# Tokens of tiles 4 to 7 transposed by DMA instead of TensorE, and the bulk of the weights issued behind them

## The chip, the core and the metric

The kernel runs on one core of a Trainium2 chip. A core has TensorE (PE: matmuls, with the weight loads that go before them, PEld), VectorE (DVE), ScalarE (ACT), GpSimd (POOL) and SyncE (SP), which issues nearly all DMAs here. Sixteen DMA engines move the data. The metric is device time of one execution in microseconds. Three runs of the kernel before took 226.38, 226.76 and 228.73 us, median 226.76.

## The reference

One layer on x of 2048 tokens by 512, bfloat16. xn is x normalised per token; to x are added a linear attention of xn with 32 heads of 16 and a gated bilinear block of xn:

```python
qkv = x @ wqkv                        # split into q, k, v of 32 heads of 16
phi = softmax(p), softmax(-p)         # p = q @ w_phi, or k @ w_phi, per head
kv  = phi_k^T v ;  z = sum_s phi_k    # over all tokens
o   = (phi_q kv) / (phi_q z + 1e-6)
A   = o @ wo
B   = ((x @ w_gate) * (x @ w_up)) @ w_down     # 512 -> 1792 -> 512
out = x + A(xn) + B(xn)
```

## The kernel before

The tokens are 16 tiles of 128. Everything stays on chip: x, the transposed normalised tokens xnT (features on the partitions, which matmuls need), all weights and the hidden values of the bilinear block.

**Tokens.** `ln` takes statistics on VectorE (L412, L414), the reciprocal root on GpSimd (L418, L420), and writes a normalised tile into a ring of four buffers, `xn_tile`, on VectorE (L434). That tile is then transposed into xnT. `emit_xn` does it in one of two ways: for tiles 0 to 7, four 128x128 matmuls against the identity into a PSUM bank (a "group") and one ScalarE copy out of it; for tiles 8 to 15, one DMA transpose issued from SP. A tile's buffer in the ring is free again when its transpose has read it.

**Keys and values.** `k_pe(t)` makes the values of a tile: four 128x512 matmuls and a ScalarE copy ("value group"). `wprime` folds w_phi into the key or query weights; it needs a weight matrix that a DMA transposes from HBM (`load_wT`, L344). `k_pk` and `k_norm` make the softmax features of the keys, with much work on VectorE (L474 and L480 for the maximum, L494 for the sums, L518, L521). `emit_kv` sums them over tokens. Later the queries go the same way, and their features and results are transposed by DMA from SP too.

**The bilinear block.** A *unit* is one of 14 slices of 128 hidden features for one of four groups of 512 tokens: a half of four 128x512 matmuls with gate, a half of four with up, a ScalarE copy of the first and a VectorE product (L543). Units 0 to 3 of a token group use the first 4 of 14 column blocks of gate and up, which are loaded early; units 4 to 13 use the other 10, the "bulk" of gate and up. Units 0 to 13 of the first token group need only tiles 0 to 3. The weights wd (w_down) and wo are used at the end, in `final`.

**Order of the work.** The program is first recorded as steps, and `_order` then sorts them by a list simulation of its own: each step has a cost, a DMA also a time `at` before which it does not count as landed, and among those ready on an engine the earliest, then that of the lowest priority number, is taken. Units have a high priority number, so they fill the gaps. The result is a fixed order for each engine. Each engine runs its list strictly in order and waits on semaphores where a step needs another engine's or a DMA's result. A dependence on a DMA is a wait for its landing. A change of a dependence, of a cost or of an `at` thus moves instructions on all engines.

**SP's queue before.** x in pieces of 1, 1, 2 tiles; the value weights wv; x of tiles 4 to 7; the first four blocks of gate and of up; the transposed load of the key weights; x of tiles 8 to 15; the bulk of gate (1280 KB) and up (1280 KB); wd (1792 KB); wo (512 KB); then the transposes of tiles 8 to 11. None of the loads waits for anything.

The functions that the diff touches:

Of the kernel before, what the change touches and what calls it, by code (L numbers as in the profile page):

```python
# [12 lines left out]
PE, ACT, DVE, POOL, SP = "PE", "ACT", "DVE", "POOL", "SP"  # L13
# [183 lines left out]
def _build(nc, es, A_x, A_wqkv, A_w_phi, A_wo, B_w_gate, B_w_up, B_w_down, out):  # L197
# [59 lines left out]
    def sbv(name, lo, n):  # L257
        off = layout[name] + lo
        return arena[:, off:off + n]
# [5 lines left out]
    def bank(b, lo=0, n=512):  # L265
        return psum[:, b * 512 + lo: b * 512 + lo + n]

    sc = _Sched(nc)


    def act_op(out_ap, in_ap, func=ACTF.Copy, scale=1.0, bias=None, prio=None):
        def fn(e):
            kw = {}
            if bias is not None:
                kw["bias"] = bias
            return e.activation(out=out_ap, in_=in_ap, func=func, scale=scale, **kw)  # L276
        r = [in_ap]
        if isinstance(scale, bass.AP):
            r.append(scale)
        if isinstance(bias, bass.AP):  # L280
            r.append(bias)
        return sc.step(ACT, fn, reads=r, writes=[out_ap], cost=(50.0 if str(in_ap.tensor.name) == "ps" else 95.0) + 0.833 * in_ap.free_size(),
                       lat=180.0, prio=prio)

    def dve(fn, reads, writes, n, rate=1.0, fixed=65.0, prio=None):
        return sc.step(DVE, fn, reads=reads, writes=writes, cost=fixed + rate * n / 0.96, lat=150.0, prio=prio)

    def pool(fn, reads, writes, n, rate=1.8, fixed=130.0, prio=None):
        return sc.step(POOL, fn, reads=reads, writes=writes, cost=fixed + rate * n, lat=120.0, prio=prio)

    def mms(items, prio=None, warm=False):

        def fn(e):
            ins = None
            for o, l, r, a, z in items:
                ins = e.matmul(o, lhsT=l, rhs=r, start=a, stop=z)  # L296
            return ins
        reads = []
        writes = []
        c = 0.0  # L300
        for o, l, r, a, z in items:
            reads += [l, r]
            writes.append(o)
            c += max(25.0, o.free_size() / 2.4 + 2.3) * (1.6 if warm else 1.0)
        return sc.step(PE, fn, reads=reads, writes=writes, cost=c, lat=260.0, prio=prio)
# [12 lines left out]
    def x_tile(t):  # L318
        return sbv("x", t * 512, 512)
# [8 lines left out]
    wo_v = sbv("wo", 0, NQ * 512).rearrange("p (q j) -> p q j", q=NQ)  # L328
    wg_v = sbv("wg", 0, NQ * FF).rearrange("p (q f) -> p q f", q=NQ)
    wu_v = sbv("wu", 0, NQ * FF).rearrange("p (q f) -> p q f", q=NQ)  # L330
    wd_v = sbv("wd", 0, NF * 512).rearrange("p (f j) -> p f j", f=NF)
# [3 lines left out]
    def load_x(on, t0, n, at):  # L335
        return sc.dma(on, sbv("x", t0 * 512, n * 512).rearrange("p (t d) -> p t d", t=n),
                      x_flat[t0 * 128:(t0 + n) * 128, :].rearrange("(t p) d -> p t d", p=128), at=at)

    def load_w(on, dst, src, at, issue=500.0):
        return sc.dma(on, dst, src, at=at, issue=issue)  # L340

    def load_wT(w, at):

        return sc.dma(SP, wT_v[:, w, :, :], A_wqkv[:, w * 512:(w + 1) * 512], transpose=True, at=at, issue=4600.0)  # L344

    def load_gu(on, f0, n, at):
        return [load_w(on, v[:, :, f0 * 128:(f0 + n) * 128],
                       src[:, f0 * 128:(f0 + n) * 128].rearrange("(q p) f -> p q f", p=128), at)
                for v, src in ((wg_v, B_w_gate), (wu_v, B_w_up))]

    sc.dma(ACT, wphi_v, bass.AP(tensor=A_w_phi.tensor, offset=A_w_phi.offset, ap=[[16, 128], [2048, NQ], [1, 16]]),
           at=4200.0)
# [5 lines left out]
    load_gu(SP, 0, 4, 10800.0)  # L358
    load_wT(1, 14000.0)
    load_x(SP, 8, 8, 17000.0)  # L360
    load_gu(SP, 4, 10, 24000.0)
    load_w(SP, wd_v, B_w_down.rearrange("(f p) j -> p f j", p=128), 30000.0)
    load_w(SP, wo_v, A_wo.rearrange("(q p) j -> p q j", p=128), 31500.0, issue=8000.0)


    zero = sbv("tree", 0, 128)
# [25 lines left out]
    def make_wbd():  # L392
        for jt in range(NQ):
            pool(lambda e, jt=jt: e.tensor_tensor(
                out=wbd_v[:, jt, :].rearrange("p (g f b) -> p g f b", g=2, b=4),
                in0=wphi_v[:, jt, None, :, None].to_broadcast([128, 2, 16, 4]),
                in1=bind8.rearrange("p (g b) -> p g b", g=2)[:, :, None, :].to_broadcast([128, 2, 16, 4]), op=ALU.mult),
                [bind8, wphi_v[:, jt, :]], [wbd_v[:, jt, :]], 128).deps.append(sc.by_eng[POOL][-2])


    stats_v = sbf("stats", 0, NT * 8).rearrange("p (t k) -> p t k", t=NT)
# [7 lines left out]
    def emit_ln_stats(t0, n):  # L409
        ts = slice(t0, t0 + n)  # L410
        for t in range(t0, t0 + n):
            dve(lambda e, t=t: e.bn_stats(stats_v[:, t, 0:6], x_tile(t)), [x_tile(t)], [stats_v[:, t, 0:6]], 512)  # L412
        for t in range(t0, t0 + n):
            dve(lambda e, t=t: e.bn_aggr(mv_v[:, t, :], stats_v[:, t, 0:6]), [stats_v[:, t, 0:6]], [mv_v[:, t, :]], 6)  # L414
        veps = lnt_v[:, 0, ts]
        var4 = mv_v[:, ts, 1:2]
        rstd4 = rstd_v[:, ts, 0:1]
        pool(lambda e: e.tensor_scalar(out=veps.unsqueeze(2), in0=var4, scalar1=1e-5, scalar2=None, op0=ALU.add),  # L418
             [mv_v[:, ts, :]], [veps], n)
        pool(lambda e: e.tensor_tensor(out=rstd4, in0=veps.unsqueeze(2), in1=mhalf[:, 0:n].unsqueeze(2), op=ALU.pow),  # L420
             [veps, mhalf], [rstd_v[:, ts, 0:1]], n, rate=155.0, fixed=400.0)

    def xn_tile(t):
        return sbv("xn", (t % 4) * 512, 512)
# [3 lines left out]
    def next_a():  # L428
        b = a_bank[0] % 5
        a_bank[0] += 1  # L430
        return b

    def emit_xn(t):
        dve(lambda e: e.tensor_scalar(out=xn_tile(t), in0=x_tile(t), scalar1=mv_v[:, t, 0:1],  # L434
                                      scalar2=rstd_v[:, t, 0:1], op0=ALU.subtract, op1=ALU.mult),
            [x_tile(t), mv_v[:, t, 0:1], rstd_v[:, t, 0:1]], [xn_tile(t)], 512, rate=0.5)
        if t >= 8:
            sc.dma(SP, xnT_v[:, :, t * 128:(t + 1) * 128], xn_tile(t), transpose=True, issue=1250.0, land=3200.0,
                   at=33000.0 + 1300.0 * (t - 8))
            return  # L440
        b = next_a()
        mms([(bank(b, q * 128, 128), xn_tile(t)[:, q * 128:(q + 1) * 128], ident, True, True) for q in range(NQ)])
        act_op(xnT_v[:, :, t * 128:(t + 1) * 128], bank(b).rearrange("p (q s) -> p q s", q=NQ))
# [106 lines left out]
    def emit_kv(half):  # L550
        for g in range(8):
            b = next_a()
            mms(group(bank(b, 0, 65), [(ek_v[:, t, g * 128:(g + 1) * 128], vext_all[:, t, g, 0:65])
                                       for t in range(half * 8, half * 8 + 8)]))
            kp = kvp_v[:, g, :]
            if half == 0:
                act_op(kp, bank(b, 0, 65))
                continue
            dve(lambda e, b=b, kp=kp: e.tensor_tensor(out=kp, in0=bank(b, 0, 65), in1=kp, op=ALU.add),  # L559
                [bank(b, 0, 65), kp], [kp], 65)  # L560
            dve(lambda e, kp=kp, g=g: e.tensor_tensor(
                out=kvx_v[:, g, 0:64].rearrange("p (h d) -> p h d", h=4),
                in0=kp[:, 0:64].rearrange("p (h d) -> p h d", h=4),
                in1=maskh[:, :, None].to_broadcast([128, 4, 16]), op=ALU.mult),
                [kp, maskh], [kvx_v[:, g, 0:64]], 64)
            dve(lambda e, kp=kp, g=g: e.scalar_tensor_tensor(
                out=kvx_v[:, g, 64:68], in0=maskh, scalar=kp[:, 64:65], in1=eps4, op0=ALU.mult, op1=ALU.add),
                [kp, maskh, eps4], [kvx_v[:, g, 64:68]], 4)
# [77 lines left out]
    def some_glu(n, g_max):  # L646
        for _ in range(n):
            if units and units[0][0] <= g_max:
                glu(*units.pop(0), (5, 6, 7) if units and units[0][0] < 3 else (5, 6))

    def ln(t0, n):
        emit_ln_stats(t0, n)
        for t in range(t0, t0 + n):
            emit_xn(t)
# [6 lines left out]
    for b0 in range(0, NT, 4):  # L661
        if b0 < 12:
            ln(b0 + 4, 4)
        if b0 == 8:
            load_wT(0, 0.0).deps.append(sc.by_eng[SP][-2])
            emit_kv(0)
            some_glu(99, 2)
        for t in range(b0, b0 + 4):
            k_pk(t)
            k_norm(t)  # L670
            if b0 < 8:
                some_glu(2, 1)
        if b0 < 12:
            for t in range(b0 + 4, b0 + 8):
                k_pe(t)
        if b0 == 8:
            wprime(0)
# [165 lines left out]
```

## Time and profile before

| | |
|---|---|
| median of three runs | 226.76 us |
| the profiled execution, its own time | 227.26 us |
| its span in the profile | 225.5 us |
| TensorE busy | 218.9 us, 97% |
| VectorE busy | 191.7 us, 85% |
| ScalarE busy | 115.5 us, 51% |
| granted TensorE clock | 0.999 |
| HBM read, written | 8.67 MB, 2.10 MB |

The profile is one execution, and all starts in it are counted from the start of its span. A row of the timeline gives start, duration, engine, line of the kernel, operation, what is written and read, and a count where like instructions are merged; in brackets the idle time of the engine before it and what ended that. SPq is SP's list of DMA issues: its duration is the time that SP was held by the issue, not that of the transfer. All matmuls have one line, L296, and all ScalarE operations L276, since helpers record them.

### The profile page before, as it was taken

How to read it: one execution, taken by the hardware profiler on the slowest of the kernel's cores; microseconds unless marked ns; L12 is line 12 of the kernel's file. 1: busy time of each engine (PE TensorE's matmuls, PEld its weight loads, DVE VectorE, ACT ScalarE, POOL GpSimd, SP SyncE). 2: the span in 40 equal slices, each digit the busy share in tenths (PEclk: the TensorE clock that was granted, in tenths of full speed). 3: DMA queues.
4: the chain of work that ended last, by engine and by line, in shares of the span. 5: the costliest groups of instructions: out<-in, count | busy, mean ns of one | idle time of the engine just before them, and what ended most of it. 6: DMA issues, size and time to landing. Idle time of an engine off the chain costs nothing.

```text
span 225.5 us, 3619 instructions
## 1 busy us (share of the span) xinstructions
PE 218.9 (97%) x1312; PEld 106.9 (47%) x1312; DVE 191.7 (85%) x548; ACT 115.5 (51%) x193; POOL 10.2 (5%) x29
## 2 busy tenths in 40 slices
PE   8899999999999999998999999989999999999995
PEld 8454444444455454443454444444444444454443
DVE  4758999999993899999989999989999999974121
ACT  2579976674434998654519765536453333100000
POOL 4721000000020000000000000000000000000000
PEclk9999999999999999999999999999999999999999
DMA  6999931300004400000000044434456643663201
GB/s 163 327 269 400 357 119 28 70 0 0 0 3 95 93 3 0 0 0 3 0 1 3 8 89 89 92 67 78 93 57 110 133 115 76 145 140 73 70 23 48
DMA packets 44210, 19.39 MB, mean 86 GB/s; under 512 B 35232, under 2 KB 43168, under 8 KB 44192
## 3 DMA queue, kind: packets, MB, share of 16 engines
q1 hardware_dynamic: 43664, 19.14, 34.5%
q8 instruction: 10, 0.16, 0.3%
q10 hardware_dynamic: 528, 0.02, 0.1%
q14 instruction: 8, 0.07, 0.1%
HBM read 8.67 MB, written 2.10 MB: 48 GB/s over the span
## 4 chain that ended last, share of the span: by engine, by line
PE 66%; DVE 20%; DMA 5%; SPq 5%; issue 2%; ACT 1%; DVEq 0%
PE ps L296 66%; DVE arena L494 4%; DVE arena L543 4%; DVE arena L474 4%; SPq L163 3%; DMA arena<-in_A_x_dram 3%; DVE arena L480 3%; DMA arena<-arena 2%; SPq L164 1%; DVE arena L412 1%; ACT arena L276 1%; DVE arena L613 1%; DVE arena L518 1%; DVE arena L599 0%; DVE arena L521 0%
## 5 line engine op out<-in xcount | busy, mean ns | idle before, releaser
L296 PE MATMUL ps<-arena 128*128 128x512 bf16 (+4 forms) x1312 | 218.9, 330 | 3.9 <-ACT arena L276 1.1
L296 PEld LDWEIGHTS ps<-arena 128*128 128x128 bf16 x1312 | 106.9, 100 | 115.7 <-ACT arena L276 6.0
L276 ACT ACTIVATE arena<-ps 128x512 bf16<-128x512 f32 (+1 forms) x160 | 84.2, 601 | 47.2 <-PE ps L296 42.3
L276 ACT ACTIVATE arena<-arena 128x1024 bf16<-128x1024 bf16 x32 | 34.3, 1074 | 32.0 <-DVE arena L480 31.1
L494 DVE TENSOR_TENSOR arena<-arena 128x512 f32<-128x512 bf16 (+3 forms) x128 | 49.3, 397 | 0.1
L543 DVE TENSOR_TENSOR arena<-ps,arena 128x512 bf16<-128x512 f32 x56 | 37.9, 679 | 3.4 <-PE ps L296 1.8
L474 DVE TENSOR_TENSOR arena<-arena 128x64 bf16<-128x64 bf16 (+3 forms) x128 | 31.5, 272 | 1.7 <-ACT arena L276 1.6
L640 DVE TENSOR_TENSOR arena<-ps,arena 128x512 bf16<-128x512 f32 (+2 forms) x17 | 11.0, 653 | 12.6 <-PE ps L296 12.5
L480 DVE TENSOR_TENSOR arena<-arena 128x1024 bf16<-128x1024 bf16 x32 | 21.7, 677 | 0.0
L412 DVE BATCH_NORM_STATS2 arena<-arena 128x6 f32<-128x512 bf16 x16 | 10.6, 683 | 4.4 <-DMA arena<-in_A_x_dram 4.4
L521 DVE TENSOR_TENSOR arena<-arena 128x1024 bf16<-128x1024 bf16 x16 | 10.9, 681 | 0.0
L613 DVE TENSOR_TENSOR arena<-ps,arena 128x512 bf16<-128x512 f32 x16 | 10.8, 672 | 0.1
L612 DVE RECIPROCAL arena<-ps 128x32 f32<-128x32 f32 x16 | 5.5, 342 | 4.6 <-PE ps L296 4.5
L518 DVE RECIPROCAL arena<-arena 128x64 bf16<-128x64 f32 x16 | 8.7, 546 | 0.1
L434 DVE TENSOR_SCALAR arena<-arena 128x512 bf16<-128x512 bf16 x16 | 6.2, 416 | 1.9 <-issue 1.5
L599 DVE TENSOR_TENSOR arena<-arena 128x512 bf16<-128x512 bf16 x16 | 6.6, 411 | 0.0
L420 POOL TENSOR_TENSOR arena<-arena 128x1 f32<-128x1 f32 (+1 forms) x7 | 5.4, 777 | 0.4
L596 DVE RECIPROCAL arena<-arena 128x32 f32<-128x32 f32 x16 | 5.4, 336 | 0.0
L418 POOL TENSOR_SCALAR arena<-arena 128x1 f32<-128x1 f32 (+1 forms) x7 | 1.7, 250 | 54.0 <-DVE arena L414 53.9
L597 DVE TENSOR_TENSOR arena<-arena 128x32 bf16<-128x32 f32 x16 | 2.8, 174 | 0.0
L559 DVE TENSOR_TENSOR arena<-ps,arena 128x65 f32<-128x65 f32 x8 | 1.4, 221 | 0.8 <-PE ps L296 0.8
L276 ACT ACT_TABLE_LOAD x1 | 1.3, 1283 | 1.3 <-PEq L828 1.3
(18 smaller groups left out, 9.8 us busy)
## 6 DMA issues: line engine op xcount, KB each, us to landing
out_dram<-arena SPq DMA_DIRECT2D x15, 128.0 KB, 1.9
arena<-in_B_w_down_dram SPq DMA_DIRECT2D x1, 1792.0 KB, 17.1
arena<-in_B_w_gate_dram SPq DMA_DIRECT2D x1, 1280.0 KB, 8.9
arena<-in_B_w_up_dram SPq DMA_DIRECT2D x1, 1280.0 KB, 12.5
arena<-in_A_x_dram SPq DMA_DIRECT2D x1, 1024.0 KB, 6.2
arena<-arena SPq DMA_TRANSPOSE x40, 2.6
arena<-in_A_wqkv_dram SPq DMA_DIRECT2D x1, 512.0 KB, 5.0
arena<-in_A_x_dram SPq DMA_DIRECT2D x1, 512.0 KB, 6.3
```

Source lines behind the costliest of these rows:

```text
L163: return e.dma_start_transpose(out_ap, in_ap)
L276: return e.activation(out=out_ap, in_=in_ap, func=func, scale=scale, **kw)
L296: ins = e.matmul(o, lhsT=l, rhs=r, start=a, stop=z)
L412: dve(lambda e, t=t: e.bn_stats(stats_v[:, t, 0:6], x_tile(t)), [x_tile(t)], [stats_v[:, t, 0:6]], 512)
L474: dve(lambda e, dst=dst, src=src, k=k: e.tensor_tensor(out=dst, in0=src[:, :, 0:k], in1=src[:, :, k:2 * k], op=ALU.max), [src], [dst], 16 ...
L480: dve(lambda e: e.tensor_tensor(out=p4, in0=p4, in1=src[:, :, None, :].to_broadcast([128, 16, 16, 4]), op=ALU.subtract), [pst, src], [pst] ...
L494: dve(lambda e, dst=dst, src=src, k=k: e.tensor_tensor(out=dst, in0=src[:, :, 0:k], in1=src[:, :, k:2 * k], op=ALU.add), [src[:, :, 0:2 * ...
L518: dve(lambda e: e.reciprocal(out=rs, in_=sm), [sm], [rs], 64, rate=6.0)
L521: dve(lambda e: e.tensor_tensor(out=e4, in0=e4, in1=r4[:, :, None, :].to_broadcast([128, 16, 16, 4]), op=ALU.mult), [ek_v[:, t, :], rs], [ ...
L543: dve(lambda e: e.tensor_tensor(out=dst, in0=bank(bu), in1=gr, op=ALU.mult), [bank(bu), gr], [dst], 512, prio=-1.0)
L613: dve(lambda e: e.tensor_tensor(out=o.rearrange("p (g h d) -> p g h d", g=8, h=4), in0=nd[:, :, 0:64].rearrange("p g (h d) -> p g h d", h= ...
L640: dve(lambda e: e.tensor_tensor(out=og, in0=ob, in1=xs, op=ALU.add), [ob, xs], [og], c1 - c0, prio=-2.0)
```

## The change

Tiles 4 to 7 take the second way of `emit_xn`: their group of four identity matmuls and the ScalarE copy go, and one DMA transpose each, issued from SP, takes their place. The three bulk loads move from the start of the program text into `load_rest`, which is called after `ln` of tiles 4 to 7. Each of its four DMAs depends on the step that is SP's last at that point, the transpose of tile 7; the first, bulk gate, so waits for the landing of that transpose, and the others stand behind it. The planned `at` times and wo's planned issue cost are set anew. SP's order after: all as before to x of tiles 8 to 15, then the transposes of tiles 4 to 7, bulk gate, bulk up, wd, wo, then the transposes of tiles 8 to 11.

```diff
     load_x(SP, 8, 8, 17000.0)
-    load_gu(SP, 4, 10, 24000.0)
-    load_w(SP, wd_v, B_w_down.rearrange("(f p) j -> p f j", p=128), 30000.0)
-    load_w(SP, wo_v, A_wo.rearrange("(q p) j -> p q j", p=128), 31500.0, issue=8000.0)
...
+    def load_rest():
+
+        queued = sc.by_eng[SP][-1]
+        late = load_gu(SP, 4, 10, 26500.0)
+        late.append(load_w(SP, wd_v, B_w_down.rearrange("(f p) j -> p f j", p=128), 32000.0))
+        late.append(load_w(SP, wo_v, A_wo.rearrange("(q p) j -> p q j", p=128), 33500.0, issue=6000.0))
+        for st in late:
+            st.deps.append(queued)
+
...
-        if t >= 8:
+        if t >= 4:
             sc.dma(SP, xnT_v[:, :, t * 128:(t + 1) * 128], xn_tile(t), transpose=True, issue=1250.0, land=3200.0,
-                   at=33000.0 + 1300.0 * (t - 8))
+                   at=35000.0 + 1300.0 * (t - 8) if t >= 8 else 19000.0 + 1300.0 * (t - 4))
             return
...
             ln(b0 + 4, 4)
+        if b0 == 0:
+            load_rest()
```

The order of instructions on TensorE changes as follows. The groups of tiles 4 to 7 are gone. Unit 1's first half stands ahead of the key weights' groups (`wprime`), and unit 2's second half ahead of the keys of tiles 0 to 3 instead of behind those of tiles 4 to 7. The value group of tile 8 stands right behind unit 6 instead of between the halves of unit 8, and those of tiles 9 to 11 move up by one to three halves with it. In the second token group a half of unit 8 changes places with the first five sums of `emit_kv`. All else is in the same order.

## The prediction

> **What bounds the kernel now.** I read the page's busy times first, then stretches of the early part, then who waited for whom, then the order of SP's issues. From the page, the busy row of TensorE and the GB/s row over 40 slices of 5.64 us:
>
> ```profile
> PE 218.9 (97%) x1312; PEld 106.9 (47%) x1312; DVE 191.7 (85%) x548; ACT 115.5 (51%) x193; POOL 10.2 (5%) x29
> GB/s 163 327 269 400 357 119 28 70 0 0 0 3 95 93 3 0 0 0 3 0 1 3 8 89 89 92 67 78 93 57 110 133 115 76 145 140 73 70 23 48
> ```
>
> TensorE is the bound: 6.6 us of idle time in 225.5. A microsecond of matmuls taken out can at best give a microsecond; a stall put in costs its length. The loads are over by slice 6 (34 us), so the change acts before about 40 us. The busy times of early stretches:
>
> ```profile
> 14.00:18.00 4.00, 3.98 (x44) 2.69 (x43) 1.81 (x6) 3.32 (x7) 0.00 (x0) 1.00 1.03 355
> 18.00:22.00 4.00, 4.00 (x20) 1.85 (x19) 4.00 (x11) 3.99 (x9) 0.53 (x2) 1.00 1.04 402
> 32.00:36.00 4.00, 4.00 (x20) 1.86 (x19) 4.00 (x11) 2.34 (x5) 0.00 (x0) 1.00 0.00 0
> 40.00:60.00 20.00, 20.00 (x95) 9.08 (x93) 20.00 (x54) 11.99 (x20) 0.00 (x0) 1.00 0.10 20
> ```
>
> The columns are PE, PEld, DVE, ACT, POOL, granted clock, DMA share, GB/s. From 14 us on TensorE has no gaps, VectorE none from 18 us on, and the DMA engines are full up to about 30 us. The clock is 1.00 throughout. The weight loads' own idle times, on the timeline, show where TensorE comes close to VectorE:
>
> ```profile
> 10.22 0.23 PEld L296 LDWEIGHTS ps<-arena 128*128 128x128 bf16 x4 [0.75 <-DVE arena L434]
> 14.24 17.01 PEld L296 LDWEIGHTS ps<-arena 128*128 128x128 bf16 x104 [0.51 <-DVE arena L434]
> 33.18 4.12 PEld L296 LDWEIGHTS ps<-arena 128*128 128x128 bf16 x20 [0.20 <-DVE arena L543]
> 37.57 0.59 PEld L296 LDWEIGHTS ps<-arena 128*128 128x128 bf16 x4 [0.27 <-ACT arena L276]
> ```
>
> SP's queue, issue by issue (start, duration):
>
> ```profile
> 4.34 7.38 SPq L163 DMA_TRANSPOSE arena<-in_A_wqkv_dram  x1
> 11.77 0.57 SPq L164 DMA_DIRECT2D arena<-in_A_x_dram  x1
> 12.39 0.58 SPq L164 DMA_DIRECT2D arena<-in_B_w_gate_dram  x1
> 14.72 9.62 SPq L164 DMA_DIRECT2D arena<-in_A_wo_dram  x1
> 73.73 1.86 SPq L163 DMA_TRANSPOSE arena<-in_A_wqkv_dram  x1
> ```
>
> The bulk's sizes and times from issue to landing:
>
> ```profile
> arena<-in_B_w_gate_dram SPq DMA_DIRECT2D x1, 1280.0 KB, 8.9
> arena<-in_B_w_up_dram SPq DMA_DIRECT2D x1, 1280.0 KB, 12.5
> arena<-in_A_wo_dram SPq DMA_DIRECT2D x1, 512.0 KB, 17.4
> ```
>
> So x of tiles 8 to 15 lands at 11.77 + 6.16 = 17.9 (6.16 from the chain that ended last), bulk gate at 21.3, bulk up at 25.5, wo at 32.1: 3.4, 7.6 and 14.2 us after that x.
>
> **What is removed.** TensorE loses four groups of four 128x128 matmuls (tiles 4 to 7). The row at 10.22 is one such group: 0.23 us, so 0.9 in all. The first of them also waited for VectorE (0.51 at 14.24, where the usual gap before a weight load in that part is 0.2 to 0.25): some 0.2 more goes. Together -1.1 us by 22 us. ScalarE loses four evictions. It does 20 in 10.02 us from 14.68 (0.5 each), so 2.0 us; TensorE waits there for nothing, so I count nothing for it. If that cover were gone the gain would still be within ScalarE's 2.0.
>
> **What is added.** Four DMA transposes stand in SP's queue behind x of tiles 8 to 15, each waiting for its normalised tile (L434, the four from 13.78 to 15.16). The bulk of gate, which stands behind them, gains a wait for the *landing* of tile 7's transpose; up, wd and wo stand behind gate, and behind them the transposes of tiles 8 to 11. Step by step:
>
> 1. Tile 4's transpose is issued at 14.2. The four transposes of tiles 8 to 11 took 1.19 to 1.49 us on SP, median 1.26, and landed 2.4 to 2.6 us after issue. Tile 7's is then issued at 14.2 + 3 x 1.26 = 18.0, just when the x ahead of it has landed (17.9), and lands at 20.6. This length is not in the trace for a queue that is still busy: from below 2.4 us (as measured idle), from above the hold that SP shows at 4.34 (rival 1). I take the idle value, the x being nearly through. TensorE asks for tiles 4 to 7 from about 21.9, 0.87 us apart (98 wide matmuls take 21.3 us from 38.77 in the chain): covered.
> 2. Bulk gate is issued at 20.7, not 12.39. The queue is empty then, so it pays a start: the first x tiles took 2.5 us for 128 KB, some 0.4 of it data at 350 GB/s, so 2.1 us. Below: the outgoing 128 KB rows, 1.9 us in all, so 1.5. Above: 2.5.
> 3. Landings: gate 20.7 + 2.1 + 3.4 = 26.2, up 30.4, wo 37.0 (before 32.1): the bulk is 4.9 us later.
> 4. TensorE reaches the first unit of bulk gate at 31.5 - 1.1 = 30.4, its up half 0.87 later at 31.3. Slack 4.2 and 0.9 us: no stall.
> 5. Tile 8's transpose comes behind wo in the same queue, though its input is ready earlier (VectorE had it by 35.9, and the new order puts it a few steps sooner). SP itself, held in wo's issue to 24.3, which is 6.4 after the x, would be free at 29.2. It lands some 0.7 after wo (its data at the same rate, and the end): 37.7. Before, TensorE's value group of tile 8 stood after the first half of unit 8; in the new order of instructions it stands two groups of unit 7 and that half earlier, right behind unit 6. That is 33.18 + 4 x 0.87 = 36.7 in the old clock, and 35.7 with the gain of 1.1 less the little that VectorE holds back at 33. **Here TensorE waits 37.7 - 35.7 = 2.0 us.**
> 6. In this wait VectorE and ScalarE catch up. The old waits at 37.57 (0.27) and 38.77 (0.61, less the usual 0.2) go: 0.4 us of TensorE at most. What is late next is tile 9's transpose, 1.26 behind tile 8's, while TensorE asks for it 2.6 behind: covered.
>
> Sum: -1.1 + 2.0 - 0.4 = **+0.5 us**. From 40 us on the order is the old one and TensorE has no gap to give it back in. The profiled execution took 227.26 (span 225.5 and 1.8 around it), so 227.8; it stands 0.5 above the median of 226.76, by which it would be 227.3. I forecast **227.6**.
>
> A rule speaks against this change: the Trainium skill, DMA: Bandwidth & Descriptors, Rules for kernel authors, says to issue a DMA early, compute meanwhile and wait late. By it the bulk's 4.9 us of delay would be a loss, and with -1.1 the sum +3.8; the rows of slack above let 2.0 of the 4.9 through.
>
> **Rivals.** (1) *SP is held at the transposes, slower.* The weight transpose at 4.34 held SP for 7.38 us with a full queue before it, and 1.86 us with an empty one at 73.73; wo's issue was held 9.62 where like issues take 0.5. If tile 4's transpose is held until x is through at 17.9, tile 7's is issued at 17.9 + 1.5 + 2 x 1.26 = 21.9 and lands at 24.4; all of steps 2 to 5 moves by 3.8, and the wait before tile 8 with it: 231.4 at the worst. If only its issue ends there, as the weight transpose's ended with the landing before it, the shift is about 2.5: 230.1. It decides from a landing of tile 7 after 22.4 (1.8 later than mine). Against it: only 1 MB is ahead, and wd's issue passed in 1.12 us with more ahead. For it: both held issues, one of them a transpose. The Trainium skill, same page, Issuing engines are not separate DMA queues, calls the sequencer's time to start a DMA usually small beside the DMA. By that this rival has no chance; the two held rows say otherwise, and I keep it.
> (2) *The wait before tile 8 is hidden.* If the start costs 1.5, tile 7 lands somewhat sooner and the bulk streams at the 400 GB/s of slice 4, tile 8 lands by 35.7. Then the gain is what VectorE allows, -0.3 to -0.9: 226.2. Against it: 4.86 MB in 14.2 us is 350 GB/s, measured.
>
> **Chances.** Forecast 0.56 (226.6 to 228.9, from the bounds of steps 1 and 2); rival 1 0.28; rival 2 0.16. The range goes from rival 2's 226.1 to 230.6, inside rival 1. A measurement of this kernel tells about 1% (2.3 us) from no change: rival 2 stays within it, so faster has 0.03, same 0.69, slower 0.28.
>
> **What would show it.** Tile 7's transpose landing near 20.6 and gate's issue right behind; wo landing near 37; a wait of TensorE for a DMA of about 2 us near 36 and none for gate or up; TensorE's count 16 lower. I am wrong if SP's transposes take much over 1.3 us each, if x of tiles 8 to 15 lands later than 17.9 (VectorE waits for it), or if up lands after 31.3.

## The result

The changed kernel took **228.38 us** (median of 6 runs, 228.0 to 228.87) against 226.74 for the kernel before, run beside it. The ratio is 1.0065, with a 95% interval of 1.0039 to 1.0091: 0.9 to 2.1 us slower. 227.6 was forecast. The profiled execution took 228.0 us, with a span of 226.3 and a granted clock of 0.999.

From the page of the changed kernel, the busy row and the GB/s row over 40 slices:

```profile
PE 217.0 (96%) x1296; PEld 105.0 (46%) x1296; DVE 191.6 (85%) x548; ACT 113.6 (50%) x189; POOL 10.2 (5%) x29
GB/s 174 324 267 91 377 358 202 28 0 0 0 0 83 107 3 0 0 0 0 3 1 0 3 93 93 68 85 83 93 70 97 132 110 77 149 136 72 72 23 48
```

TensorE has its 16 matmuls less and is 1.9 us less busy, in a longer span. Slice 4 (17 to 23 us) has fallen from 400 to 91 GB/s: the bulk of the weights now starts in it. SP's queue on the timeline, issue by issue (start, and duration of the issue; a merged row runs from its first issue to the end of its last):

```profile
4.41 6.70 SPq L163 DMA_TRANSPOSE arena<-in_A_wqkv_dram  x1
11.16 0.57 SPq L164 DMA_DIRECT2D arena<-in_A_x_dram  x1
13.53 6.15 SPq L163 DMA_TRANSPOSE arena<-arena  x4
20.91 0.38 SPq L164 DMA_DIRECT2D arena<-in_B_w_gate_dram  x1
...
23.77 5.86 SPq L164 DMA_DIRECT2D arena<-in_A_wo_dram  x1
31.60 41.69 SPq L163 DMA_TRANSPOSE arena<-arena  x8
```

The four new transposes hold SP from 13.53 to 19.68. The last lands at 20.90, and gate is issued right behind. The page's DMA issues (size, us from issue to landing):

```profile
arena<-in_B_w_gate_dram SPq DMA_DIRECT2D x1, 1280.0 KB, 6.7
arena<-in_B_w_up_dram SPq DMA_DIRECT2D x1, 1280.0 KB, 9.6
arena<-in_A_x_dram SPq DMA_DIRECT2D x1, 1024.0 KB, 7.2
...
arena<-in_A_wo_dram SPq DMA_DIRECT2D x1, 512.0 KB, 13.9
```

Gate lands at 27.57, up at 30.96, wo at 37.67 and tile 8's transpose at 38.15. The x of tiles 8 to 15, on which nothing was changed but what stands behind it in the queue, takes 7.2 us from issue to landing, where it took 6.2. The waits of TensorE's weight loads:

```profile
31.90 0.56 PEld L296 LDWEIGHTS ps<-arena 128*128 128x128 bf16 x4 [1.18 <-DMA arena<-in_B_w_up_dram]
...
34.43 1.48 PEld L296 LDWEIGHTS ps<-arena 128*128 128x128 bf16 x8 [0.25 <-DVE arena L549]
38.19 32.84 PEld L296 LDWEIGHTS ps<-arena 128*128 128x128 bf16 x188 [2.28 <-DMA arena<-arena]
```

The wait for tile 8 that was forecast is there: the last matmul ahead of it starts at 36.03, the next could follow 0.22 later, at 36.24, and it starts at 38.19: 1.95 us. A smaller one, at 31.9, was not forecast.

The row that matters most is VectorE's. The timeline of the kernel before shows, between 16 and 75 us, these idle times of VectorE, and none between the first two rows:

```profile
17.95 0.69 DVE L412 BATCH_NORM_STATS2 arena<-arena 128x6 f32<-128x512 bf16 x1 [2.19 <-DMA arena<-in_A_x_dram]
69.54 0.69 DVE L543 TENSOR_TENSOR arena<-ps,arena 128x512 bf16<-128x512 f32 x1 [1.48 <-ACT arena L276]
71.99 0.69 DVE L543 TENSOR_TENSOR arena<-ps,arena 128x512 bf16<-128x512 f32 x1 [1.76 <-PE ps L296]
73.97 1.73 DVE L474 TENSOR_TENSOR arena<-arena 128x512 bf16<-128x512 bf16 x6 [1.29 <-ACT arena L276]
```

So before, VectorE works from the landing of that x to 68 us without a gap. In the changed kernel:

```profile
16.57 0.69 DVE L549 TENSOR_TENSOR arena<-ps,arena 128x512 bf16<-128x512 f32 x1 [1.50 <-PE ps L296]
18.39 1.29 DVE L418 BATCH_NORM_STATS2 arena<-arena 128x6 f32<-128x512 bf16 x2 [1.12 <-DMA arena<-in_A_x_dram]
40.99 0.69 DVE L549 TENSOR_TENSOR arena<-ps,arena 128x512 bf16<-128x512 f32 x1 [1.46 <-PE ps L296]
70.69 0.69 DVE L549 TENSOR_TENSOR arena<-ps,arena 128x512 bf16<-128x512 f32 x1 [1.07 <-PE ps L296]
```

It starts on tile 8 at 18.39, and while TensorE stands at the wait for tile 8, no products (L549) come for it: 1.46 us are lost at 40.99. The stretches around that (columns as in the prediction):

```profile
36.00:40.00 4.00, 2.21 (x11) 0.87 (x10) 3.53 (x8) 2.20 (x4) 0.00 (x0) 1.00 0.93 112
40.00:60.00 20.00, 20.00 (x94) 9.04 (x93) 18.91 (x50) 12.05 (x20) 0.00 (x0) 1.00 0.03 7
```

VectorE had 4.00 and 20.00 in them before; now 3.53 and 18.91.

To follow the time past that, I take a mark that the kernels share in which x of tiles 8 to 15 is one load: the first ScalarE copy of the third group of tokens, which stands behind an idle time of 1.13 us. On ScalarE's timeline, of before and then of the changed kernel, it is the row at 91.02 and the first such copy at 92.65:

```profile
91.02 1.73 ACT L276 ACTIVATE arena<-ps 128x512 bf16<-128x512 f32 x3 [1.13 <-PE ps L296]
```

```profile
92.65 0.60 ACT L276 ACTIVATE arena<-ps 128x512 bf16<-128x512 f32 x1 [1.13 <-PE ps L296]
```

From VectorE's start on tile 8 to the mark it is 73.07 us before and 74.26 after. From the mark to the start of VectorE's last instruction it is 132.00 and 131.10. The difference of the two profiled executions, 228.0 - 227.26 = 0.74, is thus: x later, +0.44; the stretch from there to the mark, +1.19; the rest, -0.90. That last term is a stall of the kernel before at 148 us that the changed kernel does not show (last section).

### The profile page after: what moved, and what is told of

The parts are those of the page before. It is cut to its first block, busy times and chain, and to the rows that moved or that the text cites. A ratio compares the mean times of both kernels' runs of the same rounds, so it can differ in the third digit from the quotient of the medians.

```text
span 226.3 us, 3588 instructions
## 1 busy us (share of the span) xinstructions
PE 217.0 (96%) x1296; PEld 105.0 (46%) x1296; DVE 191.6 (85%) x548; ACT 113.6 (50%) x189; POOL 10.2 (5%) x29
## 4 chain that ended last, share of the span: by engine, by line
PE 80%; DVE 7%; DMA 6%; SPq 4%; ACT 1%; issue 1%; DVEq 0%
PE ps L296 80%; DMA arena<-in_A_x_dram 3%; SPq L163 3%; DMA arena<-arena 3%; DVE arena L480 1%; SPq L164 1%; DVE arena L418 1%; DVE arena L500 1%; DVE arena L486 1%; DVE arena L549 1%; ACT arena L276 1%; DVE arena L527 0%; DVE arena L646 0%; DVE arena L524 0%; DVE arena L440 0%
## 5 line engine op out<-in xcount | busy, mean ns | idle before, releaser
L296 PEld LDWEIGHTS ps<-arena 128*128 128x128 bf16 x1296 | 105.0, 99 | 118.3 <-ACT arena L276 6.9
L276 ACT ACTIVATE arena<-ps 128x512 bf16<-128x512 f32 (+1 forms) x156 | 82.1, 602 | 50.9 <-PE ps L296 44.7
L500 DVE TENSOR_TENSOR arena<-arena 128x128 f32<-128x128 f32 (+3 forms) x128 | 49.3, 395 | 0.2
L549 DVE TENSOR_TENSOR arena<-ps,arena 128x512 bf16<-128x512 f32 x56 | 37.9, 678 | 6.6 <-PE ps L296 6.3
L420 DVE BATCH_NORM_AGGREGATE arena<-arena 128x2 f32<-128x6 f32 x16 | 2.0, 160 | 0.0
```

What stands on the lines that cost most here:

```text
L500: dve(lambda e, dst=dst, src=src, k=k: e.tensor_tensor(out=dst, in0=src[:, :, 0:k], in1=src[:, :, k:2 * k], op=ALU.add), [src[:, :, 0:2 * ...
L549: dve(lambda e: e.tensor_tensor(out=dst, in0=bank(bu), in1=gr, op=ALU.mult), [bank(bu), gr], [dst], 512, prio=-1.0)
```

## The experiments

Each ratio is to the kernel before, run beside it on the same chip. 1% is 2.27 us.

**No wait for the landing.** The bulk of gate stays behind the four transposes in the queue, and waits only for the last VectorE step before them.

```diff
-        queued = sc.by_eng[SP][-1]
+        queued = sc.by_eng[DVE][-1]
```

> The changed kernel, but the bulk of the weights depends on the normalised tile 7 (a VectorE step) and not on the landing of its transpose, so it is issued right behind the four transposes and the queue does not run empty. Orders on all engines are those of the changed kernel. Theory A (the changed kernel loses by the wait before tile 8's value group, set by the delay of the bulk ahead of tile 8's transpose): wo lands 2 to 3 us sooner, near 35, the wait of 2 us near 36 falls below 0.5, time 226.6 to 227.3. Theory B (the four DMA transposes by themselves slow the queue, the empty queue is of no account): wo lands within 0.7 us of 37.7 and the time stays at 228.0 to 228.7.

Measured: 227.67 us, ratio 1.0044 [1.0025, 1.0063]. Gate is issued 2.0 us sooner, wo lands at 36.01, tile 8 at 36.60, and TensorE's wait for it shrinks to 0.58. Some 0.5 us come back, not all, though now nearly nothing is waited for here: x still takes 6.8 us, and TensorE stops for 0.86 us before 151.6, which it does not in the changed kernel (last section).

**wd and wo behind the transposes of tiles 8 to 11.**

```diff
-        late.append(load_w(SP, wd_v, B_w_down.rearrange("(f p) j -> p f j", p=128), 32000.0))
-        late.append(load_w(SP, wo_v, A_wo.rearrange("(q p) j -> p q j", p=128), 33500.0, issue=6000.0))
...
+    def load_last():
+
+        for st in (load_w(SP, wd_v, B_w_down.rearrange("(f p) j -> p f j", p=128), 60000.0),
+                   load_w(SP, wo_v, A_wo.rearrange("(q p) j -> p q j", p=128), 60000.0)):
+            st.deps.append(sc.by_eng[DVE][-1])
...
+        if b0 == 4:
+            load_last()
```

> The changed kernel with wd and wo issued behind the transposes of tiles 8 to 11 instead of ahead of them; the landing wait stays, gate and up stay late. TensorE's order is that of the changed kernel. Theory A: tile 8's transpose lands near 34.3, before TensorE asks for it at 36.2, no wait there, time 226.3 to 227.1; wd and wo land near 50 and nobody waits. Theory C (what costs is gate and up being late, or the evictions behind VectorE near 31, and the wait at tile 8 only shows it): 227.8 to 228.7.

Measured: 227.21 us, 1.0020 [1.0005, 1.0035]. Tile 8's transpose lands at 33.19, and nothing waits for it. That of tile 10, not forecast, lands only at 40.35; TensorE waits 0.31 us for it before 40.39, and VectorE loses 0.39 us at 42.33. The wait for tile 8 is gone, and the kernel that then has 1.1 us less work on TensorE is still no faster than before; it is, by its interval, 0.1 to 0.8 us slower. So the wait for tile 8 is a cause of the loss, and the 1.1 us show as no gain, with a small wait left that takes a part of them.

**The queue alone.** The kernel before with the new queue: the four transposes are issued into a place that is not read, the bulk waits for them, and TensorE and ScalarE make tiles 4 to 7 as before. The orders of TensorE, VectorE and ScalarE are the old ones. `load_rest` is that of the change.

```diff
...
+    scr_v = sbv("wd", 0, 4 * 512).rearrange("p (t q s) -> p t q s", t=4, q=NQ)
...
-        if t >= 8:
+        if t >= 4:
+            dst = xnT_v[:, :, t * 128:(t + 1) * 128] if t >= 8 else scr_v[:, t - 4, :, :]
+            sc.dma(SP, dst, xn_tile(t), transpose=True, issue=1250.0, land=3200.0,
+                   at=35000.0 + 1300.0 * (t - 8) if t >= 8 else 19000.0 + 1300.0 * (t - 4))
+        if t >= 8:
             return
```

> The queue of the changed kernel with the work of the kernel before: tiles 4 to 7 are transposed by TensorE into xnT as before, and besides by DMA into a place that nobody reads (the later home of wd), ahead of the bulk. TensorE's order is exactly that of the kernel before, in which the value group of tile 8 is asked for at 39.6. Theory A: tile 8's transpose lands at 38.2 as in the changed kernel, before it is asked for, and up at 31.0, before 32.4: no wait, time 226.4 to 227.2, the delay of the bulk is free in the old order. Theory D (the delay of the bulk costs by itself, wherever the value group stands): 228 or more.

Measured: 227.20 us, 1.0020 [1.0008, 1.0032]. VectorE's idle times on the timeline:

```profile
18.32 0.69 DVE L420 BATCH_NORM_STATS2 arena<-arena 128x6 f32<-128x512 bf16 x1 [3.08 <-DMA arena<-in_A_x_dram]
69.92 0.69 DVE L553 TENSOR_TENSOR arena<-ps,arena 128x512 bf16<-128x512 f32 x1 [1.48 <-PE ps L297]
```

VectorE waits 3.08 us for x instead of 2.19, starts on it 0.37 later than before, and every later row is later by that: 69.92 against 69.54. Here TensorE does all its old work and loses nothing to the wait for tile 8, whose value group stands where it stood. x took 7.2 us.

**The value groups later.** In the changed kernel, the planner's `at` of the transposes of tiles 8 to 11 is raised, so that TensorE's value groups come later.

```diff
-                   at=35000.0 + 1300.0 * (t - 8) if t >= 8 else 19000.0 + 1300.0 * (t - 4))
+                   at=38000.0 + 1300.0 * (t - 8) if t >= 8 else 19000.0 + 1300.0 * (t - 4))
```

> The changed kernel with one number of the planner changed: the transposes of tiles 8 to 11 count as landed from 38 us on and not from 35, so that the value group of tile 8 stands behind both halves of unit 8 instead of right behind unit 6. Queue and loads are those of the changed kernel. Theory A: TensorE reaches it near 39.7, 1.5 after the landing, no wait, time 226.2 to 227.1 (the saved 1.1 us less what VectorE and ScalarE hold back). Theory D: 228 or more.

Measured: 228.21 us, 1.0066 [1.0046, 1.0085], as slow as the changed kernel. VectorE has no gap from tile 8 to 69 us in it, but starts on tile 8 only at 19.09, x having taken 7.3 us, and two rows of TensorE wait for ScalarE (1.14 us before 32.63, 1.37 before 71.62). From the mark on it takes 132.5 us, 0.5 more than before and 1.4 more than the changed kernel: TensorE stops for DMA transposes before 152.8 (0.75 us) and 175.8 (0.43). So moving the groups does win back most of what the wait cost up to the mark (73.36 against 74.26), and the late x and these stops take it again: in the medians it is worth nothing.

After these four the theory was another: from the landing of x of tiles 8 to 15 to about 68 us VectorE sets the pace, and the transposes queued behind that x make it land later. The next six test the two halves of it.

**More work on TensorE.** The groups of tiles 4 to 7 twice.

```diff
-            for o, l, r, a, z in items:
+            for o, l, r, a, z in items * times:
...
+            times=2 if t >= 4 else 1)
```

> The kernel before, with the four TensorE groups that transpose tiles 4 to 7 done twice over, the second time onto the same bank. TensorE has 0.9 us more to do between 14 and 22 us; nothing else differs, and the order of every engine is the old one. It prices, with the other sign, what the change takes away. Theory that TensorE sets the pace in this stretch (the prediction's minus 1.1 us): 226.7 + 0.9 = 227.6 us. Theory that VectorE sets it from the landing of x of tiles 8 to 15 to the first sums of keys near 66 us: 226.7, at most 0.3 more.

Measured: 227.23 us, 1.0015 [0.9988, 1.0042], that is +0.3 with -0.3 to +1.0: by time alone neither theory is excluded. Its profile says more. VectorE's idle times:

```profile
17.05 0.69 DVE L412 BATCH_NORM_STATS2 arena<-arena 128x6 f32<-128x512 bf16 x1 [1.90 <-DMA arena<-in_A_x_dram]
18.01 0.69 DVE L544 TENSOR_TENSOR arena<-ps,arena 128x512 bf16<-128x512 f32 x1 [0.26 <-PE ps L296]
23.26 0.73 DVE L475 TENSOR_TENSOR arena<-arena 128x512 bf16<-128x512 bf16 x3 [0.27 <-ACT arena L276]
```

x landed early in this run, and VectorE could not use it: it waits twice, for TensorE and for a ScalarE copy behind it. The mark comes 74.15 us after the start on tile 8, 1.08 later than before. So work put on TensorE there does pass through once VectorE must wait for it; TensorE has little slack itself.

**Less work on TensorE**, the term -1.1 by itself: one matmul in place of four in these groups. It leaves out three quarters of these tiles' transposes, so that the result is not the reference's.

```diff
-            for o, l, r, a, z in items:
+            for o, l, r, a, z in items[:first]:
...
+            first=1 if t >= 4 else NQ)
```

> The kernel before, with one 128x128 matmul in place of four in each of TensorE's groups for tiles 4 to 7. It leaves out the transposes of the last three quarters of these tiles (ScalarE copies what the bank held), so what is computed of their keys is not the reference's; the order of every engine, ScalarE's copies and all loads are the old ones. TensorE has 12 matmuls of 0.058 us less between 14 and 22 us, 0.7 us. Theory that TensorE sets the pace (the prediction's minus 1.1): 226.0. Theory that VectorE, without a gap from 17.95 to 66 us, sets it: no change, 226.7 within 0.2. The run with the groups done twice cost 0.3 to 0.5 and had gaps in VectorE, 0.26 and 0.27 us, so that costs on TensorE pass on while savings would not.

Measured: 226.38 us, 0.9989 [0.9965, 1.0013]: -0.25 with -0.8 to +0.3. The profile shows where the 0.7 us go. VectorE's idle times, and then a wait of TensorE's weight loads that the kernel before does not have:

```profile
17.41 0.69 DVE L412 BATCH_NORM_STATS2 arena<-arena 128x6 f32<-128x512 bf16 x1 [2.27 <-DMA arena<-in_A_x_dram]
69.00 0.69 DVE L544 TENSOR_TENSOR arena<-ps,arena 128x512 bf16<-128x512 f32 x1 [1.48 <-PE ps L296]
```

```profile
30.95 1.42 PEld L296 LDWEIGHTS ps<-arena 128*128 128x128 bf16 x8 [0.77 <-issue]
```

TensorE is early (its copies for key tile 4 come 0.65 sooner than in a second trace of the kernel before, which has the same landing of x within 0.06), gives it back by 36 us, most of it in that row, and VectorE is where it was: 69.00 - 17.41 = 51.59 as before's 69.54 - 17.95 = 51.59. A saving on TensorE in this stretch is worth nothing. The -0.25 has, by the trace, another source: the mark is 0.28 later than in that second trace, and from there on it takes 131.04 us against 131.95, without the stall at 148 us (last section).

**x earlier.** The kernel before, with x of tiles 8 to 11 ahead of the transposing load of the key weights.

```diff
+    load_x(SP, 8, 4, 12500.0)
-    load_wT(1, 14000.0)
-    load_x(SP, 8, 8, 17000.0)
+    load_wT(1, 15000.0)
+    load_x(SP, 12, 4, 17500.0)
```

> The kernel before, with x of tiles 8 to 11 loaded ahead of the transposing load of the second group of wqkv, and x of tiles 12 to 15 alone behind it. VectorE waits 2.19 us for x of tiles 8 to 15 before 17.95 us; here it should start on tile 8 near 15 us. Theory that VectorE sets the pace from that landing to about 66 us: the end moves with it, 225 to 226 us, 1 us less at the least that its later waits leave. Theory that TensorE sets the pace there: VectorE only waits elsewhere, and the time stays at 226.7 (within 0.3).

Measured: **225.50 us**, 0.9944 [0.9932, 0.9957]: 1.0 to 1.5 us faster than before, faster than both kernels, with all of TensorE's work in place. VectorE's one idle time between 12 and 66 us, TensorE's matmuls from then on, and those of the second trace of the kernel before (below):

```profile
13.06 0.69 DVE L413 BATCH_NORM_STATS2 arena<-arena 128x6 f32<-128x512 bf16 x1 [1.37 <-DMA arena<-in_A_x_dram]
```

```profile
10.43 210.56 PE L296 MATMUL ps<-arena 128*128 128x512 bf16 x1220 [0.35 <-ACT arena L276]
```

```profile
10.53 93.71 PE L296 MATMUL ps<-arena 128*128 128x512 bf16 x514 [0.45 <-ACT arena L276]
105.00 41.63 PE L296 MATMUL ps<-arena 128*128 128x512 bf16 x262 [0.76 <-ACT arena L276]
147.36 74.76 PE L296 MATMUL ps<-arena 128*128 128x68 bf16 x444 [0.73 <-DMA arena<-arena]
```

VectorE starts on tile 8 at 13.06 instead of 17.95; TensorE then runs from 10.43 to 220.99 without a wait. But the trace does not put the gain where the theory had it. TensorE is busy for 88.41 of the first 92 us, against 88.60 in the second trace of the kernel before (both hold 1289 matmul records): 4.9 us given to VectorE win nothing there, so TensorE is a bound of this stretch as well. From 92 to 220 us it is busy for 127.21 us against 125.72, since the waits before 105 us (0.76) and 147.4 us (0.73) are gone. The first may be owed to VectorE being ahead; the second is the stall of the last section. TensorE's order is another one here, and neither was tested. So this run does not show what an earlier x is worth.

**The kernel before again**, for a second trace.

> The kernel before once more, for a second trace. If the load of x of tiles 8 to 15 takes what it takes because of what stands behind it in its queue, it lands near 6.2 us after its issue, as in the first trace of this kernel, and not at 6.5 to 7.3, as in the changed kernel and the experiments on it. If it varies from run to run, this trace may show 6.5 or more as well.

Measured: 226.67 us in the profiled execution. x takes 6.1 us; VectorE starts on tile 8 at 17.36, 0.59 sooner than in the first trace, and the mark is 0.57 sooner. All of the difference between these two executions of one kernel is in when x of tiles 8 to 15 came: its issue ended the hold by the weight transpose at 11.22 here, at 11.72 there.

**The transposes behind the landing of x.** The kernel with the new queue alone, but with the four transposes held until x has landed; gate follows without a wait.

```diff
-        queued = sc.by_eng[SP][-1]
+        queued = x8
...
+            if 4 <= t < 8:
+                st.deps.append(x8)
```

> As the kernel that transposes tiles 4 to 7 on both ways (TensorE's copy is used, the DMA's is not read), but the four DMA transposes wait for the landing of x of tiles 8 to 15, so that nothing stands in the queue behind that x; the bulk of gate follows them without a wait for their landing. Theory that the transposes queued behind x delay its landing: x lands about 6.2 us after its issue, as before, and the time falls from 227.2 back to about 226.7 (a stall of some tenths where up of the bulk is late is possible and would show at 32 us). Theory that the delay comes from elsewhere (a fetch of instructions on one ring at that time): x still takes about 7 us, and the time stays near 227.2.

Measured: 228.73 us, 1.0088 [1.0074, 1.0103]. The DMA issues of x, SP's queue, and TensorE's waits:

```profile
arena<-in_A_x_dram SPq DMA_DIRECT2D x1, 1024.0 KB, 5.7
```

```profile
11.71 0.57 SPq L165 DMA_DIRECT2D arena<-in_A_x_dram  x1
17.52 5.15 SPq L164 DMA_TRANSPOSE arena<-arena  x4
22.71 0.58 SPq L165 DMA_DIRECT2D arena<-in_B_w_gate_dram  x1
```

```profile
32.43 5.72 PEld L297 LDWEIGHTS ps<-arena 128*128 128x128 bf16 x28 [0.39 <-DMA arena<-in_B_w_up_dram]
...
40.92 19.11 PEld L297 LDWEIGHTS ps<-arena 128*128 128x128 bf16 x90 [1.90 <-DMA arena<-arena]
```

The first theory was right on x and wrong on the time, the second wrong on both. x is quick again, 5.7 us against 7.2 with the transposes queued behind it, in two kernels that differ only in these waits and in what follows the transposes. In both a fetch of 16 KB of instructions starts while x is under way, at 16.4 us here and at 16.2 there, so that the fetch is not what tells them apart. But the time rose, since the bulk now starts at 22.7: tile 8 lands at 40.88, TensorE waits for it (1.90 by its weight loads, where the changed kernel's row has 2.28; 1.58 from matmul to matmul, where that has 1.95), and the mark comes 74.84 after the start on tile 8, 1.77 later than before. This prices the wait with all old orders: 1.6 us of it, and the wait of 0.39 for up's weights ahead of it, cost 1.8.

**Three edits together.** The changed kernel with x of tiles 8 to 11 earlier, without the wait for the landing, and with wd and wo behind the transposes of tiles 8 to 11.

```diff
-    load_wT(1, 14000.0)
-    load_x(SP, 8, 8, 17000.0)
+    load_x(SP, 8, 4, 12500.0)
+    load_wT(1, 15000.0)
+    load_x(SP, 12, 4, 17500.0)
...
-        queued = sc.by_eng[SP][-1]
+        queued = sc.by_eng[DVE][-1]
...
```

> The changed kernel with three edits together: x of tiles 8 to 11 ahead of the transposing load of wqkv, the bulk of gate behind the transposes of tiles 4 to 7 in the queue but without a wait for their landing, and the loads of wd and wo behind the transposes of tiles 8 to 11. No DMA should be waited for after 18 us. Theory that VectorE sets the pace: its start on tile 8 near 13 us is worth what it was worth in the kernel before (226.7 to 225.5), and with VectorE done earlier the 1.1 us that TensorE is spared can count too: 224.4 to 225.5. If the earlier x is delayed by the transposes queued behind it, or TensorE then waits for tiles 4 to 7: 225.5 to 226.5.

Measured: 227.58 us, 1.0032 [1.0012, 1.0052], worse than its expectation. The x of tiles 12 to 15 took 5.2 us with transposes queued behind it, 3.7 without them in the kernel with x earlier alone, but VectorE did not wait for it. TensorE waits once more for a DMA transpose of tiles 8 to 11, and once near 148 us for one of the queries' transposes:

```profile
41.13 5.73 PEld L296 LDWEIGHTS ps<-arena 128*128 128x128 bf16 x28 [1.26 <-DMA arena<-arena]
...
148.17 11.89 PEld L296 LDWEIGHTS ps<-arena 128*128 128x128 bf16 x77 [1.44 <-DMA arena<-arena]
```

These two waits are 2.7 us, and the matmuls stop once more for a DMA transpose, 0.84 us before 171.1; why the later two are there I did not test. What the spared TensorE work is worth where VectorE is early stays open.

The ten traces in which x of tiles 8 to 15 is one load, in one table; the load is from issue to landing, the start is VectorE's on tile 8, the distance is from there to the mark, and the rest from the mark to the start of VectorE's last instruction:

| kernel | behind x in the queue | load of x, us | start, us | distance, us | rest, us | ratio |
|---|---|---|---|---|---|---|
| before | bulk of gate | 6.2 | 17.95 | 73.07 | 132.00 | 1 |
| before, second trace | bulk of gate | 6.1 | 17.36 | 73.10 | 131.95 | 1 |
| groups twice | bulk of gate | 5.8 | 17.05 | 74.15 | 132.12 | 1.0015 |
| one matmul of four | bulk of gate | 6.1 | 17.41 | 73.32 | 131.04 | 0.9989 |
| transposes behind the landing | nothing until 17.5 | 5.7 | 17.47 | 74.84 | 131.85 | 1.0088 |
| queue alone | transposes | 7.2 | 18.32 | 73.07 | 131.99 | 1.0020 |
| changed | transposes | 7.2 | 18.39 | 74.26 | 131.10 | 1.0065 |
| no wait for the landing | transposes | 6.8 | 18.04 | 73.11 | 132.16 | 1.0044 |
| wd and wo behind | transposes | 6.5 | 17.53 | 73.05 | 131.92 | 1.0020 |
| value groups later | transposes | 7.3 | 19.09 | 73.36 | 132.50 | 1.0066 |

Three things are seen. With the transposes queued behind it the load takes 6.5 to 7.3 us, else 5.7 to 6.2. And the distance is 73.05 to 73.36 wherever TensorE neither waits about 2 us for tile 8 nor has the groups twice, whether TensorE has the 1.1 us of work more or less. The rest is 131.0 to 131.1 in the changed kernel and the one with one matmul of four, and 131.8 to 132.5 in all others.

## Why the time came out so

- **What bounds the kernel.** The step that failed. The prediction read TensorE as the bound from its 6.6 us of idle time and took its matmuls at full price in the early stretch. The stretches that it showed had VectorE busy for all of 18 to 60 us as well. From 18 to 68 us both are full, and a gain on one alone is worth nothing. VectorE has no gap from the landing of x of tiles 8 to 15 on, so a cut on TensorE gives nothing (one matmul of four), and a later x delays all that follows (the two traces of the kernel before). TensorE has no slack either: added work passes through (groups twice), and an earlier start of VectorE won nothing ahead of 92 us (x earlier).
- **What is removed, -1.1 us by 22 us.** TensorE did get there early: it reached the first unit of bulk gate 1.40 us sooner than before, 0.3 of that by an earlier front in this trace. It was worth nothing at the end: a saving of 0.7 alone was given back by 36 us, and the kernel with the saving and without the wait (wd and wo behind) is as slow as the one with the new queue and no saving, 1.0020 each, though a wait of 0.3 us for tile 10 is in the first.
- **Step 1, the transposes.** Issue of tile 7's at 18.42 (forecast 18.0), landing at 20.90 (20.6). Right; the first took 2.2 us of SP, the others 1.26. Rival 1, SP held until x is through, did not come. What the step took for granted was wrong: x landing unchanged at 17.9. It took 1.0 us longer, and landed at 18.36 though it was issued 0.6 sooner. The prediction had named that as a thing that would make it wrong. The new queue alone, which holds this cost and no saving, measured +0.45 us (0.2 to 0.7).
- **Step 2, the start of an empty queue.** Issue at 20.91 (20.7). Gate landed 6.65 after it where 2.1 + 3.4 = 5.5 were reckoned, so the start cost 3.2 us, over the upper bound of 2.5. A like issue into an empty queue (the queue alone) landed after 6.59.
- **Step 3.** Gate 27.57 (26.2), up 30.96 (30.4), wo 37.67 (37.0): late by the start, in part made up by a faster stream behind it.
- **Step 4, no stall.** Up landed just in time, but the row of the weight load at 31.90 has 1.18 of idle time, 0.88 of it lost by the matmuls: up's half had to wait for a ScalarE copy behind one that waited for VectorE. VectorE worked on through it, so it cost nothing.
- **Step 5, tile 8.** Landing 38.15 (37.7), asked for at 36.24 (35.7), wait 1.95 (2.0). Right in mechanism, place and length. Its price is not its length: from the start on tile 8 to the mark the changed kernel loses 1.19 us, I take it because TensorE came to it early; with the old orders, 1.6 us of it and a little for up cost 1.8.
- **Step 6, -0.4 and nothing after 40 us.** Wrong. There was no 0.4 to win, the old waits being TensorE's waits for VectorE's pace (the second trace of the kernel before is without the larger of them and no shorter from the start on tile 8 to the mark), and VectorE lost 0.47 + 1.09 us in 36 to 60 us.
- **The sum.** -1.1 + 2.0 - 0.4 should have read: 0 for the saving, +0.5 for the later x (the queue alone, by its median), +1.0 for the wait (the changed kernel against wd and wo behind, 1.0065 - 1.0020). That is +1.5, as measured, but the medians hide a fourth term: the stall at 148 us, which the changed kernel is without and all three others have. The traces show it, the changed kernel's against the second of the kernel before: x later +1.03, the wait +1.16, the rest -0.85, together +1.34 (228.0 - 226.67 = 1.33). The two first traces lie only 0.74 apart, since that of before stands 0.5 over its median (its x was issued late) and that of the changed kernel 0.4 under its own. So the forecast came near by luck: a saving wrongly credited and a delay of x that was missed stood against a wait booked at more than its price, and against a stall that went away unforeseen.
- **Rival 2** had the better bound, "the gain is what VectorE allows", and gave it 0.3 to 0.9 (its 226.2 stands as 226.1 in the range). With the wait for tile 8 hidden (wd and wo behind; 0.3 us for tile 10 are left) VectorE allowed nothing.

The rule of the Trainium skill, DMA: Bandwidth & Descriptors, Rules for kernel authors, to issue DMAs early and wait late, was weighed by the bulk's delay in the prediction. The runs bear it out in part: the bulk's delay costs nearly only through the small transpose that stands behind it. x of tiles 8 to 11 issued 7.4 us sooner (4.34 against 11.77) went with 1.3 us less, but how much of that the earlier issue earned is open.

## What to carry to other kernels

Where two engines show no idle time in the same stretch, a cut on one alone is worth nothing there, while a stall or added work on it still costs. Find the last late input and see which of the two has no gap from its landing on: a delay of that input moves all that follows. Price a reordered queue by what stands in front of the moved transfers as well as by what stands behind: here a load that no edit touched came a microsecond later. And before a difference of half a per cent is put down to an edit, look in the traces for the place where it arises: the kernel with x earlier was 0.6% faster, and none of it arose before 92 us.

## What the hardware showed

- **A load is slower with DMA transposes queued behind it.** The 1 MB of x took 5.7 to 6.2 us in five traces without them and 6.5 to 7.3 in five with them. In the first trace of the kernel before the completions of its 16 parts came over 1.27 us (16.65 to 17.93); in the changed kernel within 0.17 (18.19 to 18.36), as if the early ones had to wait for the last. Making the transposes wait for the landing took the effect away; how it comes about inside the DMA engines was not seen.
- **An emptied queue is slow to fill.** 1280 KB landed 6.5 to 6.7 us after issue into an empty queue in four traces, and 6.1 and 6.3 us behind transposes that were still under way, where the stream before it and after it took 3.4 us for as much.
- **A stall that comes and goes with the program.** In both traces of the kernel before, and with the queue alone, TensorE stops near 148 us for a DMA transpose of the queries; several of the other kernels have such a row at 149 to 153 us, the one with the groups twice at 188. On TensorE's timeline of the kernel before:

```profile
147.97 57.40 PE L296 MATMUL ps<-arena 128*128 128x68 bf16 x347 [0.78 <-DMA arena<-arena]
```

The changed kernel and the one with one matmul of four show no such row; they take 131.0 to 131.1 us from the mark to the start of VectorE's last instruction, the kernel before and the queue alone 132.0. The one with x earlier has none either. In the first trace of before, a fetch of 16 KB of instructions on one DMA ring starts at 145.8 us, while that transpose is under way. The same is seen in the other traces with such a row (with the groups twice the fetch starts 0.6 us before the issue), but the fetch alone does not decide it: in the changed kernel one starts at 148.95 us, 0.5 after a transpose is issued, and that transpose lands 3.6 us after its issue, where those waited for in these rows took 4.5 to 4.9. The cause stays open. Some 0.9 us of any comparison of two versions of this kernel can come from there.
